# Two orders for the first loads and key tiles, and two ways to store the last half tile, in a gated mix of linear attention and a token MLP

## The chip, the cores and the metric

The kernel runs on one core of one Trainium2 chip. The metric is the device time of one execution in microseconds (us). The kernel before takes 166.1 us, the median of three runs that lie between 165.94 and 166.13 us.

## The reference

The input x has 2048 rows of 512 values in bf16. Branch A is linear attention with 32 heads of 16 values, branch B normalises each row and mixes along the rows with a two-layer MLP of 1792 hidden units, and a gate per row mixes the two.

```
x = A_x                                            # 2048 x 512
g = sigmoid((x * gate_w).sum(-1))                  # one gate per row
q, k, v = split(x @ wqkv)                          # 32 heads of 16
phi = lambda t: where(t > 0, t + 1, exp(t)) + 1e-6
kv  = sum over rows of phi(k)^T v                  # per head
z   = sum over rows of phi(k)
a   = (phi(q) @ kv) / (phi(q) @ z + 1e-6) @ wo
h   = layernorm(x)
u   = gelu(h^T @ w1 + b1)
b   = (u @ w2 + b2)^T
out = g * a + (1 - g) * b
```

## The kernel before, in words

The 2048 rows are 16 tiles of 128 rows (`NT`), the 512 columns are 4 chunks of 128 (`ND`). TensorE contracts over partitions, so x is needed as it is (`xs`) and transposed (`xT`). All engines run the order in which the instructions are written (`manual_schedule`); there is no scheduler. Across engines the order is kept by semaphores.

**The head.** The first loads have 128 KB each: x tiles 0 to 3 (`load_x`, line 124) and the four chunks of Wk (`load_wk`, line 127). They are issued half on SyncE's DMA ring (SP) and half on ScalarE's (ACT), four each. Before, SP carries x tile 0, Wk chunk 0, x tile 3, Wk chunk 2, and ACT carries x tiles 1 and 2 and Wk chunks 1 and 3. Behind them SP issues DMA transposes for the rest of `xT` (`load_xT`, line 130) and all larger loads. While the first loads are under way, TensorE runs six warm-up matmuls on a constant (`warm_up`, tile `wps`). Then `transpose_tile` (line 194) transposes x tiles 0 to 3 on TensorE into `pt`, and VectorE (tiles 0 and 2, line 200) or ScalarE (tiles 1 and 3, line 198) copies them to `xT`.

**The K stage.** `k_part(t, ks)` adds the products of `xT` and Wk for the given chunks to the accumulator `kacc` of key tile t, four matmuls of 128x512 for a whole tile. `k_phi(t)` makes phi of it: ScalarE takes the exponential (line 204), and VectorE does two instructions (lines 205 and 208), the second of which writes `pk`. `g_tile(t)` then adds four matmuls of x tile t with `pk` tile t to the four accumulators `gacc`. Key tiles 0 to 3 (`HEADS`) are written out by hand. From tile 4 a loop issues `k_part(t)`, `k_phi(t)` and `g_tile(t - 4)`, and on VectorE one layer-norm step (`ln_step`, line 228) per tile. After the loop `g_tile(12)` to `g_tile(15)` follow, and `gacc` is copied to `gT` (lines 312 and 314).

In the hand-written part before, TensorE transposes tiles 0, 1 and 2, does chunks 0 and 1 of key tiles 0 to 2, transposes tile 3, and then finishes key tiles 0, 1 and 2 one by one with chunks 2 and 3, each followed by its phi. Tile 3 is done last, with all four chunks.

**The middle.** 224 matmuls `uacc` make the hidden units, with the query blocks (`qacc`), the attention's small products and the weights' streams beside them.

**The last stage.** For each of 16 row tiles TensorE does 4 matmuls `aps` and 14 matmuls `yps`, ScalarE makes `a_sc` (line 457), VectorE mixes (line 472) and SP stores (line 476). The last tile is done in two halves of 256 columns, each with a store of its own.

Of the kernel before, what the change touches and what calls it, by code (L numbers as in the profile page):

```python
# [15 lines left out]
def kernel(  # L16
# [13 lines left out]
    nc = tc.nc  # L30
    P = nc.NUM_PARTITIONS
# [9 lines left out]
    ND = D // P  # L41
# [9 lines left out]
    o_view = O.rearrange("(t p) d -> p t d", p=P)  # L51
# [15 lines left out]
    def bank(name, dtype=FP32):  # L67
        return ps.tile([P, SC], dtype, name=name, tag="bank")
# [38 lines left out]
    def mm(o, lhsT, rhs, start, stop, **kw):  # L107
        nc.tensor.matmul(o, lhsT=lhsT, rhs=rhs, start=start, stop=stop, **kw)  # L108
# [14 lines left out]
    def load_x(q, t0, n):  # L123
        q.dma_start(out=xs[:, t0 : t0 + n, :], in_=x_view[:, t0 : t0 + n, :])

    def load_wk(q, k):
        q.dma_start(out=wk_sb[:, k, :], in_=wqkv_view[:, k, D : 2 * D])

    def load_xT(t0, n):
        nc.sync.dma_start(  # L130
            out=xT[:, :, t0 * P : (t0 + n) * P], in_=X[t0 * P : (t0 + n) * P, :], transpose=True
        )

    load_x(nc.sync, 0, 1)
    load_x(nc.scalar, 1, 1)
    load_wk(nc.sync, 0)
    load_x(nc.scalar, 2, 1)
    load_x(nc.sync, 3, 1)
    for k, q in ((1, nc.scalar), (2, nc.sync), (3, nc.scalar)):
        load_wk(q, k)  # L140
    load_xT(4, 2)
    load_xT(6, 2)
    load_x(nc.sync, 4, 4)
# [5 lines left out]
    for c, (j0, nb) in enumerate(w1_chunks):  # L149
        w = wpool.tile([P, NT, FB * P], BF16, name="w1c", tag="wc")  # L150
        w1c.append(w)
        for t0 in range(0, NT, 8) if c == 0 else (0,):
            t1 = t0 + 8 if c == 0 else NT
            nc.sync.dma_start(
                out=w[:, t0:t1, : nb * P], in_=w1_view[:, t0:t1, j0 * P : (j0 + nb) * P]
# [10 lines left out]
        out=ident[:], in_=ident[:], compare_op=ALU.not_equal, fill=1.0, base=0,  # L166
# [16 lines left out]
    def warm_up(n, cols=SC):  # L183
        for _ in range(n):
            mm(wps[:, :cols], warm[:, 0:P], warm[:, :cols], True, True)
# [5 lines left out]
    def transpose_tile(t, on_act):  # L191
        pt = bank("pt", BF16)
        for k in range(ND):
            nc.tensor.transpose(pt[:, k * P : (k + 1) * P], xs[:, t, k * P : (k + 1) * P], ident[:])  # L194
        dst = xT[:, :, t * P : (t + 1) * P]
        src = pt[:].rearrange("p (k s) -> p k s", k=ND)
        if on_act:
            nc.scalar.activation(out=dst, in_=src, func=ACT.Copy)  # L198
        else:
            nc.vector.tensor_copy(out=dst, in_=src)  # L200
# [13 lines left out]
    def k_part(t, ks):  # L214
        if t not in kaccs:
            kaccs[t] = bank("kacc")
        for k in ks:
            mm(
                kaccs[t][:], xT[:, k, t * P : (t + 1) * P], wk_sb[:, k, :],
                k == 0, k == ND - 1,  # L220
            )

    def k_phi(t):
        phi(pk[:, t, :], kaccs.pop(t))

    def ln_stats(t):
        stats = work.tile([P, nc.vector.BN_STATS_DIM], FP32, name="stats", tag="stats", bufs=2)
        nc.vector.bn_stats(out=stats[:], in_=xs[:, t, :])  # L228
        nc.vector.bn_aggr(out=mv[:, t, :], in_=stats[:])

    def ln_rstd(g):
        s = slice(g * TPC, (g + 1) * TPC)
        nc.vector.tensor_scalar_add(out=veps[:, s], in0=mv[:, s, 1], scalar1=EPS)
        nc.gpsimd.tensor_tensor(out=rstd[:, s], in0=veps[:, s], in1=mhalf[:], op=ALU.pow)
# [36 lines left out]
    def ln_step(u):  # L271
        ln_stats(u)
        if u % TPC == TPC - 1:
            ln_rstd(u // TPC)

    HEADS = 4
    transpose_tile(0, False)
    transpose_tile(1, True)
    transpose_tile(2, False)
    ln_step(0)  # L280
    for k in range(2):
        for t in range(HEADS - 1):
            k_part(t, (k,))
    transpose_tile(HEADS - 1, True)
    ln_step(1)
    for t in range(HEADS):
        k_part(t, range(2 if t < HEADS - 1 else 0, ND))
        k_phi(t)
    LAG = 4
    LN_LAG = 3  # L290
# [116 lines left out]
    def rden_chunk(c):  # L407
        if c == 0:
            nc.gpsimd.dma_start(out=rd_dram[:], in_=rden[:])
        for j in range(ND):  # L410
            rex = work.tile([P, SC], BF16, name="rex", tag="rex", bufs=4)
            src = rd_dram[32 * c + 8 * j : 32 * c + 8 * j + 8, :]
            nc.gpsimd.dma_start(out=rex[:], in_=src.unsqueeze(1).to_broadcast([8, HEAD, SC]))  # L413
            seg = pqT[:, j, c * SC : (c + 1) * SC]
            nc.vector.tensor_tensor(out=seg, in0=seg, in1=rex[:], op=ALU.mult)  # L415
# [8 lines left out]
    for j in range(NB0, NF):  # L424
# [19 lines left out]
        out=gg[:], in0=gth[:], scalar1=0.5, scalar2=0.5, op0=ALU.mult, op1=ALU.add  # L444
    )
    nc.vector.tensor_scalar(
        out=c1[:], in0=gth[:], scalar1=-0.5, scalar2=0.5, op0=ALU.mult, op1=ALU.add
# [3 lines left out]
    for t in range(NT):  # L451
        c, tl = divmod(t, TPC)
        aps = bank("aps")
        for j in range(ND):
            mm(aps[:], pqT[:, j, t * P : (t + 1) * P], W2sb[:, j, :], j == 0, j == ND - 1)
        a_sc = work.tile([P, D], FP32, name="a_sc", tag="a_sc", bufs=2)
        nc.scalar.activation(  # L457
            out=a_sc[:], in_=aps[:], func=ACT.Identity,
            scale=gg[:, t : t + 1], bias=c2[:, t : t + 1],
        )  # L460
        parts = 2 if t == NT - 1 else 1
        W = D // parts
        for h in range(parts):
            cs = slice(h * W, (h + 1) * W)
            yps = bank("yps")
            for f in range(NF):
                mm(
                    yps[:, :W], w2c[c][:, f, tl * P : (tl + 1) * P], uT[:, f, cs],
                    f == 0, f == NF - 1,
                )  # L470
            ot = opool.tile([P, D], BF16, name="ot", tag="ot")
            nc.vector.scalar_tensor_tensor(  # L472
                out=ot[:, :W], in0=yps[:, :W], scalar=c1[:, t : t + 1], in1=a_sc[:, cs],
                op0=ALU.mult, op1=ALU.add,
            )
            nc.sync.dma_start(out=o_view[:, t, cs], in_=ot[:, :W])
        if 0 < t < NSC - 1:
            rden_chunk(t + 1)

# [29 lines left out]
```

## Time and profile before

| | |
|---|---|
| time, median of 3 runs | 166.1 us (165.94 to 166.13) |
| the profiled execution | 166.13 us, of which the span is 164.0 us |
| TensorE (PE) busy | 158.9 us, 97% of the span |
| VectorE (DVE) busy | 87.8 us, 54% |
| ScalarE (ACT) busy | 58.7 us, 36% |
| GpSimd (POOL) busy | 18.3 us, 11% |
| granted TensorE clock | 1.0 |

How to read the views: L108 is line 108 of the kernel. A timeline row has the start, the time, the engine, line and operation, the tile written and the tiles read, and how many instructions were merged; in brackets stands how long the engine was idle before it and what ended that. SPq and ACTq are instructions that only issue DMAs. A row of the waits has who waited for whom, the total, how often, and the longest. The row of a stretch has its length and then the busy time of PE, PEld (weight loads), DVE, ACT and POOL, the granted clock, the share of DMA and GB/s. Matmuls overlap: one of 128x512 is shown with 379 ns, but the next starts 216 ns later.

### The profile page before, as it was taken

The numbers are of one execution on the slowest core, as the hardware profiler recorded it, in microseconds if no ns is written. First come the engines' busy times: TensorE is split into PE (matmuls) and PEld (weight loads), VectorE is DVE, ScalarE is ACT, GpSimd is POOL, SyncE is SP. The second block draws the span as 40 slices with busy tenths as digits, with TensorE's granted clock in tenths as the row PEclk, the third lists the DMA queues.
The fourth block names the chain that finished last, engine by engine and source line by source line (L and its number), as shares of the span: only waits on it lengthen the run. The fifth ranks groups of instructions, "written<-read, shape, count | busy, mean of one in ns | idle before, by whom it ended". The sixth has DMA issues, their size and how long they took to land.

```text
span 164.0 us, 2057 instructions
## 1 busy us (share of the span) xinstructions
PE 158.9 (97%) x771; PEld 74.1 (45%) x785; DVE 87.8 (54%) x200; ACT 58.7 (36%) x90; POOL 18.3 (11%) x37
## 2 busy tenths in 40 slices
PE   7999999999999999999999999999999999999992
PEld 2544444444544444434444444444444444444471
DVE  0599999958999999009994401256211111111131
ACT  3463386658577373212322113111122221111110
POOL 5000710200200000001055500050000000000000
PEclk9999999999999999999999999999999999999999
DMA  4999999999930005800993599932010011101001
GB/s 147 242 213 252 288 297 356 350 348 349 317 86 0 0 0 184 268 0 0 288 293 91 182 306 297 326 129 79 32 36 32 32 36 50 42 32 36 32 32 32
DMA packets 29993, 25.05 MB, mean 153 GB/s; under 512 B 7776, under 2 KB 29408, under 8 KB 29984
## 3 DMA queue, kind: packets, MB, share of 16 engines
q1 hardware_dynamic: 27968, 22.02, 45.0%
q0 software_dynamic: 1440, 2.38, 5.3%
q10 hardware_dynamic: 576, 0.52, 1.1%
q8 instruction: 6, 0.10, 0.3%
q14 instruction: 3, 0.02, 0.0%
HBM read 21.11 MB, written 2.23 MB: 142 GB/s over the span
## 4 chain that ended last, share of the span: by engine, by line
PE 95%; DMA 2%; issue 1%; ACT 0%; DVE 0%
PE uacc L108 29%; PE yps L108 29%; PE qacc L108 8%; PE gacc L108 8%; PE aps L108 8%; PE kacc L108 8%; DMA xs<-in_A_x_dram 2%; PE pt L194 1%; PE denps L108 1%; PE kvps L108 1%; PE wps L108 1%; ACT xT L198 0%; DVE ot L472 0%; PE zps L108 0%; PE pt L323 0%
## 5 line engine op out<-in xcount | busy, mean ns | idle before, releaser
L108 PE MATMUL uacc<-hs,w1c 128*128 128x512 bf16 x218 | 51.6, 379 | 0.4
L108 PE MATMUL yps<-uT,w2c 128*128 128x512 bf16 (+1 forms) x235 | 50.8, 366 | 0.2
L472 DVE SCALAR_TENSOR_TENSOR ot<-yps,c,a_sc 128x512 bf16<-128x512 f32 (+1 forms) x17 | 12.2, 719 | 46.1 <-PE yps L108 46.1
L108 PEld LDWEIGHTS <-w2c 128*128 128x128 bf16 x238 | 23.3, 98 | 25.3
L108 PEld LDWEIGHTS <-w1c 128*128 128x128 bf16 x224 | 21.6, 98 | 26.1 <-issue 0.4
L457 ACT ACTIVATE a_sc<-aps,c,gg 128x512 f32<-128x512 f32 x16 | 12.4, 778 | 46.7 <-PE aps L108 43.0
L317 ACT ACTIVATE uT<-uacc,bcol 128x512 bf16<-128x512 f32 x14 | 9.3, 687 | 27.7 <-PE uacc L108 27.7
L108 PE MATMUL qacc<-xT,wq_sb 128*128 128x512 bf16 x64 | 16.4, 379 | 0.0
L108 PE MATMUL aps<-W2sb,pqT 128*128 128x512 bf16 x62 | 16.2, 379 | 0.1
L108 PE MATMUL kacc<-wk_sb,xT 128*128 128x512 bf16 x63 | 15.9, 379 | 0.1
L108 PE MATMUL gacc<-pk,xs 128*128 128x512 bf16 x62 | 15.5, 379 | 0.1
L244 ACT ACTIVATE hs<-xs,nmr,rstd 128x512 bf16<-128x512 bf16 x16 | 12.8, 804 | 1.9 <-DVE nmr L238 1.9
L204 ACT ACTIVATE e<-qacc 128x512 bf16<-128x512 f32 x16 | 9.6, 597 | 10.1 <-PE qacc L108 10.1
L413 POOL DMA_DIRECT2D rex<-rd_dram x16 | 9.5, 603 | 23.0 <-DVE pqT L415 18.1
L204 ACT ACTIVATE e<-kacc 128x512 bf16<-128x512 f32 x16 | 9.3, 595 | 6.9 <-PE kacc L108 5.6
L208 DVE SCALAR_TENSOR_TENSOR pk<-kacc,e 128x512 bf16<-128x512 f32 x16 | 11.1, 692 | 0.6
L208 DVE SCALAR_TENSOR_TENSOR pqT<-qacc,e 128x512 bf16<-128x512 f32 x16 | 11.1, 692 | 0.6
L228 DVE BATCH_NORM_STATS2 stats<-xs 128x6 f32<-128x512 bf16 x16 | 10.9, 682 | 0.0
L205 DVE TENSOR_SCALAR e<-e 128x512 bf16<-128x512 bf16 x32 | 9.0, 281 | 3.1 <-ACT e L204 3.1
L400 DVE CUSTOM_DVE_ANT_0 junk<-xs,gw_b 128x512 bf16<-128x512 bf16 x16 | 9.8, 683 | 0.0
L108 PEld LDWEIGHTS <-xs 128*128 128x128 bf16 x64 | 6.3, 98 | 7.5
L108 PEld LDWEIGHTS <-pqT 128*128 128x128 bf16 x64 | 6.3, 98 | 7.6
(64 smaller groups left out, 73.2 us busy)
## 6 DMA issues: line engine op xcount, KB each, us to landing
w2c<-in_B_w_dram SPq DMA_DIRECT2D x4, 1792.0 KB, 8.8
w1c<-in_B_w_dram SPq DMA_DIRECT2D x2, 2048.0 KB, 15.5
w1c<-in_B_w_dram SPq DMA_DIRECT2D x3, 1024.0 KB, 12.3
rex<-rd_dram POOLq DMA_DIRECT2D x16, 128.0 KB, 2.9
out_dram<-ot SPq DMA_DIRECT2D x15, 128.0 KB, 1.7
xs<-in_A_x_dram SPq DMA_DIRECT2D x3, 512.0 KB, 5.3
wq_sb<-in_A_wqkv_dram SPq DMA_DIRECT2D x1, 512.0 KB, 6.9
wv_sb<-in_A_wqkv_dram SPq DMA_DIRECT2D x1, 512.0 KB, 10.9
```

The costliest lines, as they stand in the source:

```text
L108: nc.tensor.matmul(o, lhsT=lhsT, rhs=rhs, start=start, stop=stop, **kw)
L194: nc.tensor.transpose(pt[:, k * P : (k + 1) * P], xs[:, t, k * P : (k + 1) * P], ident[:])
L204: nc.scalar.activation(out=e[:], in_=acc[:], func=ACT.Exp)
L205: nc.vector.tensor_scalar(out=e[:], in0=e[:], scalar1=1.0, scalar2=PHI_EPS, op0=ALU.min, op1=ALU.add)
L208: nc.vector.scalar_tensor_tensor(out=dst, in0=acc[:], scalar=0.0, in1=e[:], op0=ALU.max, op1=ALU.add)
L228: nc.vector.bn_stats(out=stats[:], in_=xs[:, t, :])
L244: nc.scalar.activation(out=hs[:, t, :], in_=xs[:, t, :], func=ACT.Identity, scale=rstd[:, t : t + 1], bias=nmr[:, t : t + 1],)
L317: nc.scalar.activation(out=uT[:, j, :], in_=acc[:], func=ACT.Gelu_apprx_tanh, bias=bcol[:, j : j + 1])
L400: nc.vector.tensor_tensor_reduce(out=junk[:], in0=xs[:, t, :], in1=gw_b[:], scale=1.0, scalar=0.0, op0=ALU.mult, op1=ALU.add, accum_out=gp ...
L413: nc.gpsimd.dma_start(out=rex[:], in_=src.unsqueeze(1).to_broadcast([8, HEAD, SC]))
L457: nc.scalar.activation(out=a_sc[:], in_=aps[:], func=ACT.Identity, scale=gg[:, t : t + 1], bias=c2[:, t : t + 1],)
L472: nc.vector.scalar_tensor_tensor(out=ot[:, :W], in0=yps[:, :W], scalar=c1[:, t : t + 1], in1=a_sc[:, cs], op0=ALU.mult, op1=ALU.add,)
```

## The change

The change has two parts.

In the head, SP now carries x tiles 0 and 2 and Wk chunks 0 and 2, and ACT carries x tiles 1 and 3 and Wk chunks 1 and 3, so that all four x tiles are ahead of all Wk chunks. TensorE transposes all four tiles first, with one warm-up matmul of 256 columns between the second and the third. Then it goes through the chunks one after the other, each for key tiles 0 to 3. The four phi follow after the last chunk.

In the last stage, the store of the last half tile (128 partitions by 256 columns) is split: partitions 0 to 63 go out on SP, partitions 64 to 127 on ACT.

```
-    load_x(nc.sync, 0, 1)
-    load_x(nc.scalar, 1, 1)
-    load_wk(nc.sync, 0)
-    load_x(nc.scalar, 2, 1)
-    load_x(nc.sync, 3, 1)
-    for k, q in ((1, nc.scalar), (2, nc.sync), (3, nc.scalar)):
-        load_wk(q, k)
+    for i in range(2):
+        load_x(nc.sync, 2 * i, 1)
+        load_x(nc.scalar, 2 * i + 1, 1)
+    for i in range(2):
+        load_wk(nc.sync, 2 * i)
+        load_wk(nc.scalar, 2 * i + 1)
...
     transpose_tile(0, False)
     transpose_tile(1, True)
+    warm_up(1, 256)
     transpose_tile(2, False)
+    transpose_tile(3, True)
     ln_step(0)
-    for k in range(2):
-        for t in range(HEADS - 1):
+    ln_step(1)
+    for k in range(ND - 1):
+        for t in range(HEADS):
             k_part(t, (k,))
-    transpose_tile(HEADS - 1, True)
-    ln_step(1)
     for t in range(HEADS):
-        k_part(t, range(2 if t < HEADS - 1 else 0, ND))
+        k_part(t, (ND - 1,))
+    for t in range(HEADS):
         k_phi(t)
...
-            nc.sync.dma_start(out=o_view[:, t, cs], in_=ot[:, :W])
+            if h < parts - 1 or parts == 1:
+                nc.sync.dma_start(out=o_view[:, t, cs], in_=ot[:, :W])
+            else:
+                nc.sync.dma_start(out=o_view[0 : P // 2, t, cs], in_=ot[0 : P // 2, :W])
+                nc.scalar.dma_start(out=o_view[P // 2 : P, t, cs], in_=ot[P // 2 : P, :W])
```

## The prediction

> **What bounds the kernel now.** I read the page first, then the chain that ended last in order of time, then the timeline of the first 14 us and of 28 to 34 us, then the waits of VectorE, and last the DMA issues at the two ends. On the page TensorE is busy for 158.9 of 164.0 us. The chain says the same:
>
> ```profile
> PE 95%; DMA 2%; issue 1%; ACT 0%; DVE 0%
> 0.81 2.92 DMA xs<-in_A_x_dram
> ...
> 5.50 1.25 PE kacc L108 x5
> 6.75 0.22 PE pt L194 x4
> 6.97 3.02 PE kacc L108 x14
> 10.00 0.86 PE gacc L108 x4
> ```
>
> The chain enters TensorE early and never leaves it before 160.77, so a delay of TensorE anywhere after 10 us goes into the end in full. 14 matmuls in 3.02 us is 0.216 us each. The change acts in two places: the first 10 us, and the last store.
>
> In the head the loads decide. In the DMA answer for issues between 1.5 and 2.1 us (last column: us from issue to landing), beside the timeline of SyncE's queue:
>
> ```profile
> xs<-in_A_x_dram ACTq DMA_DIRECT2D x1, 128.0 KB, 2.9
> wk_sb<-in_A_wqkv_dram SPq DMA_DIRECT2D x1, 128.0 KB, 3.1
> wk_sb<-in_A_wqkv_dram ACTq DMA_DIRECT2D x1, 128.0 KB, 4.1
> xs<-in_A_x_dram SPq DMA_DIRECT2D x1, 128.0 KB, 4.3
> ```
>
> ```profile
> 1.27 0.43 SPq L127 DMA_DIRECT2D wk_sb<-in_A_wqkv_dram  x1
> 1.75 0.43 SPq L124 DMA_DIRECT2D xs<-in_A_x_dram  x1
> 2.23 0.44 SPq L127 DMA_DIRECT2D wk_sb<-in_A_wqkv_dram  x1
> ```
>
> All eight loads have 128 KB, so I take landing by place in the ring: second on SP (Wk chunk 0) 1.27 + 3.1 = 4.4, third on SP (x tile 3) 1.75 + 4.3 = 6.05, fourth on SP (2.23 + 4.5 in its own answer) 6.7; on ACT second 4.1, third 1.71 + 4.1 = 5.8, fourth 6.5.
>
> What I looked for next is who else depends on the head. The timeline at 7 to 9 us, then VectorE's complete list of waits from 8.1 to 32.8 us (the whole K stage), then its busy time in stretches of that stage (third number after PE and PEld):
>
> ```profile
> 7.50 1.08 ACT L204 ACTIVATE e<-kacc 128x512 bf16<-128x512 f32 x2
> 8.13 0.29 DVE L205 TENSOR_SCALAR e<-e 128x512 bf16<-128x512 bf16 x1 [0.89 <-ACT e L204]
> ```
>
> ```profile
> DVE e L205 <- ACT e L204: 0.9, 1, 0.9
> ```
>
> ```profile
> 8.10:12.20 4.10, 4.05 (x19) 1.86 (x19) 3.90 (x10) 2.61 (x5) 0.00 (x0) 1.00 1.05 206
> 24.50:28.60 4.10, 4.10 (x20) 1.86 (x19) 3.96 (x11) 2.59 (x5) 0.34 (x1) 1.00 1.04 351
> ```
>
> VectorE waits once, for the exponential of key tile 0 at 8.13, and then works without a gap through the stage, beside a full TensorE. So it is a second bound: its last key tile lands when it started plus a fixed length. How much room is there? At the stage's end (timelines of 28.8 to 34.6 us and of TensorE around 32.4):
>
> ```profile
> 31.12 0.69 DVE L208 SCALAR_TENSOR_TENSOR pk<-kacc,e 128x512 bf16<-128x512 f32 x1
> ...
> 32.70 1.09 ACT L314 ACTIVATE gT<-gacc 128x512 bf16<-128x512 f32 x2 [1.55 <-PE gacc L108]
> ```
>
> ```profile
> 32.06 0.81 PE L108 MATMUL gacc<-pk,xs 128*128 128x512 bf16 x3
> ```
>
> The last phi is done at 31.12 + 0.69 = 31.81. The four gacc matmuls of tile 15, which need it, begin with the second of the row, 32.06 + 0.216 = 32.28. With 0.05 for the handover (ACT's xT copy ends at 5.45, TensorE goes on at 5.50) the slack is only 0.42 us.
>
> **The change part by part.**
>
> *Load order.* Nothing is added, but Wk chunk 0 goes from second to third place on SP and x tiles 2 and 3 each take a second place. So x tiles 0 to 3 are there by 4.4 us, and chunk 0 by 6.05 instead of 4.4. Chunks 1, 2, 3 land at 5.8, 6.7, 6.5 and are used later than that. SyncE's later queue (the xT transposes, from 3.56) waits on the first loads as before; nothing moves there.
>
> *TensorE's order.* All four transposes come first, with one more warm-up matmul of 256 columns: half of a cold 512-column one (rows of wps: start to start 0.43), so 0.21 us. Tiles 0 and 1 end at 4.6, the warm-up at 4.8, tiles 2 and 3 at about 5.3. Their copies (DVE 0.42, ACT 0.60) end at 5.8 and 6.1. All of this lies under the wait for chunk 0 and costs nothing. If chunk 0 came at once, the copies would be the limit: the first kacc could begin at 5.33 and tile 3's at 6.18, which counts as a start of 5.53.
>
> *First kacc.* 6.05 + 0.04 = 6.09 (0.04 is what tile 0's transposes took from the landing of x, 3.73 to 3.77). Before, the 20 kacc matmuls of tiles 0 to 4 ended at 9.83 (14 from 6.81). Now they end at 6.09 + 20 x 0.216 = 10.41. On TensorE alone that is 0.57 later.
>
> *First phi.* The order by chunk finishes tile 0 with its 13th matmul, where before it took the 8th, which ran at 7.03. It starts at 6.09 + 12 x 0.216 = 8.68. The exponential follows 0.42 later (a last kacc at 13.07 and its e at 13.49), 9.10; VectorE 0.62 after that (7.50 to 8.13), 9.72. So VectorE's unbroken chain begins 1.59 later than at 8.13. Its instructions and their order are unchanged, so tile 15's phi is done at 33.40 and gacc of tile 15 starts at 33.45, against 32.28: **+1.17 us**. On the way gacc of tile 0 waits for the first phi (9.72 + 1.02 + 0.05 = 10.79, 0.38 after TensorE is free), which puts TensorE 0.95 late; that lies inside the 1.17 and is not added. Later exponentials come 0.95 late against VectorE's 1.59, so VectorE never waits for them.
>
> After the stage TensorE's chain is unbroken to the end and its other helpers follow it with the same lag, so nothing gives this back.
>
> *Last store.* The last multiply-add ends at 161.28, the store is issued at 161.31 and lands 1.5 us later. Now SP and ACT carry 64 partitions each. Answers of the DMA view for the third-last and the last store:
>
> ```profile
> out_dram<-ot SPq DMA_DIRECT2D x1, 128.0 KB, 1.7
> ```
>
> ```profile
> out_dram<-ot SPq DMA_DIRECT2D x1, 64.0 KB, 1.5
> ```
>
> Halving the bytes took 0.2 off, but with half as many columns; the two halves together still carry 64 KB. No row shows half the partitions. Bounds: a gain of 0.77 if the whole 1.5 went with the partitions, a loss of 0.2 if ACT's ring or the second completion is later (the head's first loads land at 3.5 on ACT and 3.7 on SP). Nearest are the two rows above, so I take a small gain, 0.05. ACT has nothing behind this issue; its last a_sc is done at 158.5.
>
> The Trainium skill (DMA: Bandwidth & Descriptors, Rules for kernel authors) speaks against this edit: two transfers of disjoint partition halves share the same 16 engines and bring nothing. By that rule the term is 0, and the sum is 0.05 higher.
>
> **Sum.** Profiled execution 166.13 (span 164.0 and 2.1 around it) + 1.17 - 0.05 = 167.25; that execution is 0.03 above the median of 166.10. I predict 167.2.
>
> **The rivals.**
>
> *TensorE alone counts* (VectorE's lateness is absorbed). Then 0.57, or 0.95 with the wait for the first phi: 166.65 to 167.05. Against it: no gap in VectorE's rows that could absorb 1.59. Chance 0.12.
>
> *Chunk 0 lands elsewhere than its place says.* At 5.3 or before, the copies limit: a start of 5.53 instead of 6.09, 0.56 less, 166.7. At the fourth place's 6.7 it is 0.65 more, 167.9. For it: the jump from 4.4 to 6.05 between second and third place is larger than any other, so a stall may sit there that need not return. Chance 0.15, both ways.
>
> *The clock falls* in TensorE's new gap, 5.3 to 6.1. At half speed (0.43 a matmul) the 20 kacc would cost 4.3 us more: 170 or above. The row that speaks against it is the gap of 0.28 before 5.50, after which the step was still 0.216; no longer gap is in the trace while the clock is up. Chance 0.02. The Trainium skill (TensorE: Matmul & The Clock Gate, What's actually happening) lets the clock fall only after an idle window of about 3.4 us; by it this rival costs nothing.
>
> *Not slower: the last store.* Its wait is the only stretch in which no engine works, so each tenth saved counts in full. It decides if the head costs its least, 0.61 (1.17 - 0.56), and the saving is its bound of 0.77: 165.97, no change. Faster by over 0.2% would need still more. Against it: 128 KB needs only 0.2 more than 64 KB, so most of the 1.5 is not in the amount. Chance 0.07 for no change, 0.04 for faster.
>
> **How the numbers follow.** My case has 0.60: 167.2. Slower by over 0.2% (0.33 us, about what a measurement of this kernel can tell from no change) holds in it and in the three rivals above the last: 0.60 + 0.12 + 0.15 + 0.02 = 0.89; same 0.07; faster 0.04. The range 166.5 to 167.9 takes in the early and the late chunk 0, and of the last store half its possible gain with an early chunk.
>
> **What would show it.** Right: first kacc at about 6.1 with TensorE idle before it, first L205 of VectorE on e at 9.7, no gap on VectorE until 33, gacc of tile 15 behind a wait for VectorE at 33.4, the end of TensorE 1.2 later. Wrong: a first kacc before 5.7; a gap in VectorE during the K stage; last halves that land within 1.2 us of issue, or after 1.7.

## The result, and the profile after

The changed kernel takes 167.77 us (median of 6 runs, 167.69 to 167.93) against 166.12 us for the kernel before in the same comparison (6 runs, 165.94 to 166.49). The ratio is 1.0098, with a 95% interval from 1.0085 to 1.0111. The forecast was 167.2, range 166.5 to 167.9. The time went up as forecast, but one term of the sum had the wrong sign and another was too large; the experiments separate them. The profiled execution took 167.86 us, 165.8 of it span; TensorE is busy 159.7 us.

The head first. The chain that ended last, in order of time, in the kernel after (start, time, what):

```profile
1.73 4.25 DMA wk_sb<-in_A_wqkv_dram
5.98 0.04 issue
6.02 3.14 PE kacc L108 x13
9.16 0.02 issue
9.18 0.60 ACT e L203
...
9.81 0.30 DVE e L204
...
10.14 0.70 DVE pk L207
10.84 0.04 issue
10.88 1.02 PE gacc L108 x4
```

Before, this stretch of the chain was TensorE alone. Now it goes from Wk chunk 0, which lands at 5.98, through the 13 matmuls that finish key tile 0, to the exponential, to VectorE and back to TensorE, which waits for the first phi. VectorE's list of waits from 8.1 to 35 us has one row again, and the timeline shows where its work begins and ends (compare 8.13 and 31.12 before):

```profile
DVE e L204 <- ACT e L203: 2.6, 1, 2.6
```

```profile
9.81 0.29 DVE L204 TENSOR_SCALAR e<-e 128x512 bf16<-128x512 bf16 x1 [2.64 <-ACT e L203]
...
32.80 0.69 DVE L207 SCALAR_TENSOR_TENSOR pk<-kacc,e 128x512 bf16<-128x512 f32 x1
33.95 1.08 ACT L315 ACTIVATE gT<-gacc 128x512 bf16<-128x512 f32 x2 [1.13 <-PE gacc L108]
```

From the start of the first of these instructions to the start of the last it is 22.99 us, as before (31.12 - 8.13). The copy of gacc, which is released by tile 15's matmuls, comes at 33.95 instead of 32.70: 1.25 later. That whole delay is still there at the end of TensorE's work. The last multiply-add begins at 162.06, before at 160.80. Now the end. In the timeline of the kernel before it is:

```profile
160.80 0.48 DVE L472 SCALAR_TENSOR_TENSOR ot<-yps,c,a_sc 128x256 bf16<-128x256 f32 x1 [0.99 <-PE yps L108]
161.31 0.33 SPq L476 DMA_DIRECT2D out_dram<-ot  x1
```

In the timeline of the kernel after, and in its DMA answer:

```profile
162.06 0.48 DVE L473 SCALAR_TENSOR_TENSOR ot<-yps,c,a_sc 128x256 bf16<-128x256 f32 x1 [0.99 <-PE yps L108]
162.57 0.56 SPq L480 DMA_DIRECT2D out_dram<-ot  x1
162.57 0.55 ACTq L481 DMA_DIRECT2D out_dram<-ot  x1
```

```profile
out_dram<-ot SPq DMA_DIRECT2D x1, 32.0 KB, 1.9
out_dram<-ot ACTq DMA_DIRECT2D x1, 32.0 KB, 2.1
```

Half the bytes on each ring, and each store takes longer: 0.56 to issue instead of 0.33, and 1.9 and 2.1 us to land instead of 1.5. From the end of the last multiply-add to the end of the span it is 3.3 us (165.8 - 162.54) instead of 2.7. So the span's 1.8 us are 1.25 from the head and 0.6 from the last store.

### The profile page after: what moved, and what is told of

It reads as the page before. It is cut to its first block, busy times and chain, and to the rows that moved or that the text cites. A ratio compares the mean times of both kernels' runs of the same rounds, so it can differ in the third digit from the quotient of the medians.

```text
span 165.8 us, 2061 instructions
## 1 busy us (share of the span) xinstructions
PE 159.7 (96%) x772; PEld 74.5 (45%) x786; DVE 87.5 (53%) x200; ACT 58.5 (35%) x90; POOL 18.2 (11%) x37
## 4 chain that ended last, share of the span: by engine, by line
PE 93%; DMA 3%; DVE 1%; issue 1%; SPq 0%; ACT 0%
PE yps L108 29%; PE uacc L108 29%; PE gacc L108 8%; PE qacc L108 8%; PE aps L108 8%; PE kacc L108 8%; DMA wk_sb<-in_A_wqkv_dram 3%; PE denps L108 1%; PE kvps L108 1%; PE wps L108 1%; SPq L124 0%; DVE pk L207 0%; ACT e L203 0%; DVE ot L473 0%; DVE e L204 0%
## 5 line engine op out<-in xcount | busy, mean ns | idle before, releaser
L108 PEld LDWEIGHTS <-xT 128*128 128x128 bf16 x64 | 6.3, 99 | 8.2 <-issue 0.8
```

## The experiments

Two questions were left: whether the head's lateness goes through VectorE, and why the split store is slow. In the code, three dots stand for lines that are not shown. Below, "the end" is the time from the end of the last multiply-add to the end of the span, 2.7 us in the kernel before.

**1. The split alone**

```
 kernel before, with the changed store:
+ nc.sync.dma_start(out=o_view[0 : P // 2, t, cs], in_=ot[0 : P // 2, :W])
+ nc.scalar.dma_start(out=o_view[P // 2 : P, t, cs], in_=ot[P // 2 : P, :W])
```

> The kernel before with the split of the last store alone. In the changed kernel the last store landed 2.1 us after issue instead of 1.5, 0.6 later. If that belongs to the split, this kernel is slower by 0.5 to 0.6 us (166.7), its head is that of before, and both issues take about 0.55 us. If the lateness came from the changed head (other rings, other queue states), the time is that of before within 0.2 us.

Measured: 166.97 us against 166.28, ratio 1.0032 (1.0019 to 1.0046). Both issues take 0.56, the stores land after 1.8 and 2.1, and the end is 3.3 us. The loss belongs to the split.

**2. The head alone**

```
 changed kernel, with the store of before:
+ nc.sync.dma_start(out=o_view[:, t, cs], in_=ot[:, :W])
```

> The change without the split: new order of loads and key tiles, one last store on SP. If the two parts add, this kernel is slower by 1.1 to 1.3 us (167.3), the last store lands 1.5 us after issue, and gacc of tile 15 starts about 1.2 us later than before, right behind the last phi. If the parts are entangled, it is slower by 0.5 or less, or by all of 1.65.

Measured: 167.21 against 166.28, ratio 1.0045 (1.0030 to 1.0059). The end is 2.7 us again. The medians of the two parts are 0.69 and 0.93 above before, 1.62 together, and the change costs 1.65: the parts add. The head's 0.93 is less than the 1.25 between the two profiles, for a reason that comes with the tenth kernel. The chain that ended last shows the wait of TensorE at the end of the K stage as a step between tiles 14 and 15:

```profile
29.96 3.45 PE gacc L108 x16
33.41 0.00 issue
33.42 1.02 PE gacc L108 x4
```

The last phi of this run begins at 32.67 and is done at 33.36.

**3. Both halves on SP**

```
 the kernel of experiment 1, with both halves on SP:
- nc.scalar.dma_start(out=o_view[P // 2 : P, t, cs], ...)
+ nc.sync.dma_start(out=o_view[P // 2 : P, t, cs], ...)
```

> The kernel before with the same two halves of 64 partitions, both issued on SP, one after the other. Theory of the collision (SP and ACT issue at the same moment and hinder each other): the first issue takes 0.33 us or less, the second follows 0.3 later, the second half lands 1.5 after its own issue, and the kernel is slower by 0.2 to 0.35 us. Theory of the half (a store of 64 partitions takes 0.55 to issue and 2 us to land by itself): the two issues take 0.55 each, and the kernel is slower by 1.0 us or more.

Measured: 167.09 against 166.28, ratio 1.0038 (1.0023 to 1.0053). The two issues, with no other DMA beside them, take as long as on two rings:

```profile
161.54 0.55 SPq L479 DMA_DIRECT2D out_dram<-ot  x1
162.15 0.58 SPq L480 DMA_DIRECT2D out_dram<-ot  x1
```

Each lands 1.9 after its issue, the end is 3.6 instead of 2.7. This speaks for the half itself, against the collision. The time expected for it (1.0 us or more) was not reached: the medians differ by 0.8, the ends of the two profiles by 0.9. A half lands after 1.9 and not after the 2 that this reckoned with.

**4. The whole store on ACT**

```
 kernel before, in place of its store:
+ q = nc.sync if h < parts - 1 or parts == 1 else nc.scalar
+ q.dma_start(out=o_view[:, t, cs], in_=ot[:, :W])
```

> The kernel before with the whole last half tile, 128 partitions, stored on ACT instead of SP. If ACT's ring is late in itself (in the changed kernel its half landed 0.25 after SP's half), this kernel is slower by 0.25 us or more. By the theory of the collision the issue takes 0.33 us and the store lands after 1.5, and the time is that of before within 0.15 us.

Measured: 166.33 against 166.28, ratio 0.9999 (0.9987 to 1.0011). The issue takes 0.35, the store lands after 1.6. So ACT's ring by itself does not explain the loss.

**5. One half only**

```
 the kernel of experiment 1, without its second half:
- nc.scalar.dma_start(out=o_view[P // 2 : P, t, cs], in_=ot[P // 2 : P, :W])
```

> The kernel before with only partitions 0 to 63 of the last half tile stored, on SP; the other 64 partitions of it are left out. So far: one store of 128 partitions takes 0.33 us to issue and lands 1.53 after the start of its issue; two stores of 64, one after the other on SP, take 0.55 and 0.58 and land after 1.85 and 1.88; on two rings at once they land after 1.86 and 2.11. Theory of the form (64 partitions cost more whoever else is there): issue 0.55, landing 1.85, although only 32 KB move. Theory of the pair (it takes two DMAs close together): issue 0.33 or less, landing 1.5 or less.

One run, read by its profile. A single store of 64 partitions, alone on SP:

```profile
161.53 0.56 SPq L479 DMA_DIRECT2D out_dram<-ot  x1
```

```profile
out_dram<-ot SPq DMA_DIRECT2D x1, 32.0 KB, 1.9
```

The end is 3.0 us. So half of the 0.6 is this form of store, with nothing beside it. The other half came with the second store at the same time: in the first experiment the end is 3.3.

**6. Two parts by columns**

```
 kernel before, in place of its last store:
+ nc.sync.dma_start(out=o_view[:, t, D // 2 : D // 2 + P], in_=ot[:, 0:P])
+ nc.scalar.dma_start(out=o_view[:, t, D // 2 + P : D], in_=ot[:, P : 2 * P])
```

> The kernel before with the last half tile stored in two parts by columns, 128 partitions by 128 columns each, one on SP and one on ACT at once. Theory of the form: both issues take 0.33 to 0.4 us; the first lands after 1.5 to 1.6, the second up to 0.25 later because there are two, and the kernel is slower by 0 to 0.3 us. Theory of the pair: both issues take 0.55, the later lands after 2.1, and the kernel is slower by 0.6 us as with the split by partitions.

Measured: 166.36 against 166.25, ratio 1.0007 (0.9996 to 1.0018). The issues take 0.33 and 0.37, the stores land after 1.5 (SP) and 1.7 (ACT), and the end is 2.8. The same 32 KB on each ring, in the same moment, but over 128 partitions, cost 0.1 instead of 0.6 and bring nothing either.

**7. More work on VectorE in the K stage**

```
         if t > LAG:
             ln_step(t - LN_LAG)
+        if t in (6, 9):
...
+            nc.vector.bn_stats(out=extra[:], in_=xs[:, 0, :])
```

> The kernel before with two more BATCH_NORM_STATS of 128x512 on VectorE in the K stage (with tiles 6 and 9), whose results nobody reads. They add 2 x 0.61 us (start to start, from the rows of the profile) to VectorE's chain. Theory that VectorE's chain decides above a slack of 0.42: the last phi is done 24.9 us after the first L205 instead of 23.7, gacc of tile 15 waits for it, and the kernel is slower by 0.8 us. Theory that TensorE alone counts: no change.

Measured: 167.24 against 166.25, ratio 1.0058 (1.0043 to 1.0073), which is 0.7 to 1.2 us; expected 0.8. From the first phi instruction (8.48) to the last it is 24.18 us instead of 22.99, 1.19 more for two instructions that nobody waits for by themselves. The chain that ended last now passes through VectorE:

```profile
32.66 0.70 DVE pk L208
33.36 0.04 issue
33.41 1.02 PE gacc L108 x4
```

So VectorE's chain decides the stage as soon as it is later than its slack. This is the step that the forecast of the head rests on.

**8. The changed head, key tiles finished one by one**

```
 kernel of experiment 2:
-    for k in range(ND - 1):
+    for k in range(2):
         for t in range(HEADS):
             k_part(t, (k,))
     for t in range(HEADS):
-        k_part(t, (ND - 1,))
-    for t in range(HEADS):
+        k_part(t, range(2, ND))
         k_phi(t)
```

> The changed head, one last store, but key tiles finished one by one: chunks 0 and 1 for tiles 0 to 3, then chunks 2 and 3 of tile 0 and its phi, of tile 1 and its phi, and so on. Tile 0 is finished by the 10th kacc matmul instead of the 13th, so VectorE's chain begins 3 x 0.216 = 0.65 us earlier than in the head-only kernel, at about 9.1. If the order by chunk costs through VectorE's chain, the kernel is about 0.5 us faster than head-only (166.7), and what is left over before, 0.3 to 0.4, is the late Wk chunk 0. If the order of the loads alone is to blame, it is as slow as head-only (167.2).

Measured: 166.41 against 166.25, ratio 1.0016 (1.0004 to 1.0029). VectorE's first phi instruction in the timeline of the head-only kernel and of this one:

```profile
9.67 0.29 DVE L204 TENSOR_SCALAR e<-e 128x512 bf16<-128x512 bf16 x1 [2.85 <-ACT e L203]
```

```profile
8.73 0.29 DVE L204 TENSOR_SCALAR e<-e 128x512 bf16<-128x512 bf16 x1 [2.10 <-ACT e L203]
```

It begins 0.94 earlier: 0.65 is the order, as worked out, and the rest is the first kacc, which began at 5.74 and not at 6.04. Most of the head's loss (ratio 1.0045 with the order by chunk) is the order of the matmuls, which made VectorE start late. What is left, 0.04% to 0.29%, or 0.16 us between the medians where 0.3 to 0.4 was expected, belongs to the rest of this head: the order of the loads, the transposes done ahead, the added warm-up, and key tile 0 finished by the 10th kacc matmul and not by the 8th. These were not tried apart.

**9. Stores of many cuts, beside TensorE's work**

```
 kernel before, in place of its store:
+ forms = {4: (64, 64), 5: (32, 96), 6: (96, 32), 7: (64, 64), 8: (32, 32, 32, 32), 9: (16, 112), 10: (112, 16)}
...
+ for n in forms.get(t, (P,)):      # tile 7 on ACT, the others on SP
+     q.dma_start(out=o_view[r0 : r0 + n, t, cs], in_=ot[r0 : r0 + n, :W])
```

> The kernel before with the stores of tiles 4 to 10 cut by partitions in several ways, beside TensorE's work: 64+64, 32+96, 96+32, 64+64 on ACT, 4 times 32, 16+112, 112+16; all of 1 KB a partition. Read in it is how long each issue takes and when it lands. If only the full 128 partitions have the short issue of 0.33, all cut ones take about 0.55. If the number of partitions decides, issue times grow or fall steadily with it. The time itself should stay that of before within 0.3 us, since all this lies under TensorE.

One run. The first issue of tiles 4, 5, 6 and 8 in the timeline of SyncE's queue, with 64, 32, 96 and 32 partitions of 1 KB:

```profile
119.34 0.56 SPq L480 DMA_DIRECT2D out_dram<-ot  x1
...
123.22 0.35 SPq L480 DMA_DIRECT2D out_dram<-ot  x1
...
127.11 0.32 SPq L480 DMA_DIRECT2D out_dram<-ot  x1
...
134.88 0.32 SPq L480 DMA_DIRECT2D out_dram<-ot  x1
```

They land after 2.0, 1.5, 1.7 and 1.4 us. 16 and 112 partitions take 0.32 as a first issue and about 0.42 right behind another one, and 64 on ACT take 0.53. Both expectations are wrong: neither is only the full 128 short, nor does the time go with the number. Of the sizes tried, 64 alone is slow, on either ring. The single time, 166.60, is 0.42 above the median of before and misses the 0.3 that was allowed. 0.2 of it lies behind the last store, which here is that of before: the end is 2.9 instead of 2.7. Why the end was longer here is not known.

**10. The first DMA transposes held back**

```
 kernel before, GpSimd's masks moved ahead of this:
...
+    nc.gpsimd.tensor_copy(out=xT[:, 0, 4 * P : 4 * P + 1], in_=xs[:, 3, 0:1])
+    nc.gpsimd.tensor_copy(out=xT[:, 0, 6 * P : 6 * P + 1], in_=wk_sb[:, 2, 0:1])
     load_xT(4, 2)
     load_xT(6, 2)
```

> The kernel before with the first two DMA transposes of x held back on SyncE until x tile 3 and Wk chunk 2 are there (GpSimd copies one column in each region after those loads, and its masks are made first). If these transposes, issued at 3.6 us, are what delays the third and fourth loads of each ring (5.8 to 6.7 us against 4.4 for the second), those now land by 5.3 and 5.8. If the loads delay each other, they land as before, 5.8 to 6.7. Either way the transposed tiles 4 and 5 come late, about 9.5 instead of 7.6, so the time may rise by up to 1 us.

One run. The transposes are issued at 6.32 instead of 3.56, and the third loads of the rings take as long as in the kernel before (4.3 on SP, 4.2 instead of 4.1 on ACT), as does the fourth on SP (4.5):

```profile
wk_sb<-in_A_wqkv_dram ACTq DMA_DIRECT2D x1, 128.0 KB, 4.2
xs<-in_A_x_dram SPq DMA_DIRECT2D x1, 128.0 KB, 4.3
```

So the transposes are not what delays them. That the eight loads delay each other fits, but was not shown further. The time, 167.07, shows the price of late transposed tiles: the chain waits for xT until 9.80.

This kernel and the nine others with the head's loads and key tiles as before also show how far that head varies by itself. VectorE's first phi instruction begins at 8.13 in the profile that the forecast used, and at 8.28 to 8.73 in these ten; with the changed head it begins at 9.81 and 9.67. Against the middle of the eleven, 8.48, the change is 1.2 to 1.3 later, and less the slack of 0.42 that is 0.8 to 0.9, close to the 0.93 of the head-only kernel. The profile of before was an early one.

One length ties these runs together. From the start of the first phi instruction to the start of the last multiply-add it is 152.66 to 152.73 us in the nine kernels whose head and K stage are those of before, early and late ones alike. With the changed head it is 152.25 and 152.26, that is 0.41 or 0.42 less, which is the slack that the forecast read. In the seventh kernel it is 153.44, 0.77 more, which is its 1.19 less the same slack.

**11. 96 and 32 partitions**

```
 kernel before, in place of its last store:
+ nc.sync.dma_start(out=o_view[0:96, t, cs], in_=ot[0:96, :W])
+ nc.scalar.dma_start(out=o_view[96:P, t, cs], in_=ot[96:P, :W])
```

> The kernel before with the last half tile stored as in the change, on SP and ACT at once, but cut into 96 and 32 partitions instead of 64 and 64. In the run with several cuts only the stores of exactly 64 partitions took 0.55 us to issue; those of 16, 32, 96 and 112 took 0.31 to 0.43. If 64 is what costs on the path, both issues here take 0.31 to 0.4 us, the later store lands after 1.5 to 1.7, and the kernel is slower by 0 to 0.2 us. If any cut by partitions over two rings costs, it is slower by 0.5 to 0.7 us as the split into halves.

Measured: 166.53 against 166.36, ratio 1.0010 (0.9999 to 1.0021). The issues take 0.35 and 0.38, the stores land after 1.6 and 1.8, the end is 2.9. On the path too, the cut at 64 costs 0.4 more than the cut at 96, and the better cut still has no gain: the later of two stores at once lands after 1.8 though it carries 16 KB.

**12. A version with a shorter end**

```
-        parts = 2 if t == NT - 1 else 1
+        for cs in (slice(0, D - P), slice(D - P, D)) if t == NT - 1 else (slice(0, D),):
...
+            n = 2 if 8 <= t < 12 else 1        # four more stores, 128 partitions by 256 columns
...
```

> The kernel before with another end. The last tile is cut into 384 and 128 columns, so that the last multiply-add and the last store are for 128 columns of all 128 partitions; and the stores of tiles 8 to 11 are each issued as two of 128 partitions by 256 columns, beside TensorE's work, which makes the last store use the semaphore that SyncE looks at last. Expected from the rows so far: the last multiply-add 0.13 us shorter than 0.48; the last store lands after 1.48 instead of 1.53; after its landing SyncE has no four more semaphores to look at (4 x 0.06). Sum 0.35 to 0.45 us faster, 165.9, if none of the pieces is hidden by another. If 14 matmuls of 128 columns are held up by their weight loads (98 ns each), up to 0.5 of it is lost again.

Measured: 165.90 against 166.18, ratio 0.9980 (0.9966 to 0.9993), faster than both kernels. The last multiply-add takes 0.35 instead of 0.48 and the end is 2.4 instead of 2.7 (161.27 + 0.35 to 164.0):

```profile
161.27 0.35 DVE L470 SCALAR_TENSOR_TENSOR ot<-yps,c,a_sc 128x128 bf16<-128x128 f32 x1
```

The two differences together are 0.43, as expected; the 0.28 of the medians lies below it, with 0.1 to 0.6 in the interval. TensorE lost nothing to the 14 short matmuls: from VectorE's first phi instruction to the end of the last multiply-add it is 153.0 us, in the kernel before 153.15. The trace of SyncE's queue tells the pieces of the end apart. After the last store has landed, SyncE looks at the remaining semaphores one after another. In the kernel before it makes five such looks, from 162.86 to 163.10, 0.06 apart; in this version the last store has the semaphore that is looked at last, and there is one look, at 163.13. From the last look to the end of the span it is 0.9 in both. So the four looks saved are 0.24 of the 0.3, and the earlier landing is the remaining 0.07.

## Why the prediction was right or wrong

*Wk chunk 0 by its place*: right. Forecast 6.05, measured 5.98. All four x tiles were there by 4.3 in this profile; in the head-only run the last of them came only at 5.0 (3.8 after its issue instead of 3.0), still ahead of chunk 0, so it cost nothing.

*First kacc and first phi*: right but for a detail. Kacc began at 6.02 (6.09 forecast). The 13 matmuls and the way to the exponential took 3.16 (6.02 to 9.18) instead of 12 x 0.216 + 0.42 = 3.01, because the first matmul's step was 0.37. VectorE began at 9.81 (9.72).

*VectorE's unbroken chain decides*: right, and shown by the seventh kernel, not only by the fit. TensorE's idle time inside the stage (0.38 forecast, 10.41 to 10.79; it went on at 10.88) was not added and did not count.

*The head's +1.17*: 1.25 between the two profiles, but 0.93 between medians. The step behind the difference is the start of the sum: it took the landings and the matmul steps of one profiled execution as the kernel's, and that execution's first phi was the earliest of eleven. In eight of the other ten, Wk chunk 1 (third on ACT) landed 4.3 to 4.6 us after its issue instead of 4.1, and the matmul that needs it began at 6.09 to 6.42 instead of 5.94. In the other two (experiments 10 and 12) it landed after 4.2 and 4.0, but the first kacc matmuls were about 0.4 apart until 6.3, where the forecast's profile has 0.216 from 5.50 on. The time of that profile, 166.13, gave no sign of it.

*The last store's -0.05*: wrong, and the measured +0.6 lies outside the bounds of -0.77 to +0.2. The step that failed is "nearest are the two rows above": a row for half the columns was taken for half the partitions, the issue time was not let grow at all, and the landing by at most 0.2. A landing after 1.7 was named as a sign of being wrong, and 1.9 and 2.1 came. Half of the 0.6 is a store of 64 partitions, which has a longer issue and landing by itself (fifth kernel), and half came with two stores at once. The rule of the Trainium skill (DMA: Bandwidth & Descriptors, Rules for kernel authors), to use one transfer of 128 partitions instead of two of disjoint halves, was the better guide: every split of the last half tile here lost, or changed nothing that could be measured. By it the term would have been 0, which is nearer but not right, and its ground, that the two halves share the same engines, cannot cover the 0.3 that one half costs alone.

*The rivals*: TensorE alone would have given 0.57 or 0.95 and is refuted by the seventh kernel; the head's 0.93 looks like the latter, and without that experiment the wrong cause would have fitted. An early or late chunk 0 exists, but small: 5.7 to 6.0 in the three profiles with the changed order of loads. The clock did not fall in the gap, which is 0.50 us long in the timeline. In this execution TensorE had not even reached its full speed before it: the eight transposes ahead of the gap took 1.06 us, where experiment 8 has 0.70, the first kacc step was 0.37, and from the second on it was 0.216. No run here shows what a gap of several microseconds would cost. The last store moved against its rival.

That the time landed within the range is in part luck. The head was forecast too large for a usual run and the end too small, 1.17 - 0.05 against 0.93 + 0.69, and the two errors have opposite signs. Had the head cost its 1.17 beside the same end, the time would have been 166.10 + 1.17 + 0.69 = 167.96, just outside the range.

## What to carry to other kernels

Look at which engine runs without a gap beside the one that the chain names: its start time, not its share of the span, decides how much a late start costs, and its slack is read from the last handover of the stage. Here no cut of the last store over two rings gained anything. What shortened the end was a shorter last multiply-add (0.13) and, more than that, a last store on the semaphore that is looked at last (0.24); the smaller store itself brought only 0.07. Before a forecast of tenths of a microsecond, compare the landings in several executions: here the first phi began anywhere from 8.13 to 8.73 in one and the same head.

## What was not expected of the hardware

A store of exactly 64 partitions took 0.53 to 0.60 us to issue, on SP and on ACT, alone or in pairs, with 512 bytes or 1 KB a partition, and landed about 0.3 later than one of 128 partitions with twice the bytes; 16, 32, 96, 112 and 128 partitions took 0.31 to 0.43. Why is open; other sizes were not tried. Of two stores issued at the same moment on SP and ACT, the one on ACT landed 0.2 to 0.3 later, whatever the cut; alone, a store on ACT landed 0.1 later than on SP (1.6 against 1.5). At the end of the program SyncE looked at one semaphore after another, 0.06 us each, so that the place of the last store's semaphore in this order was worth up to 0.24 us.
